# Attention and MLP in one kernel: batch 1's q exponentials by token tile, w1's sums in the raw weights' place, w2's differences in smaller parts, steps placed later

## The chip, the cores and the metric

The kernel runs on one core of a Trainium2 chip. The metric is the time on the device in microseconds (us), the median of a few runs. One execution was also taken by the hardware profiler. Engines are named as in its page: PE (TensorE), DVE (VectorE), ACT (ScalarE), POOL (GpSimd), SP (SyncE). Each runs its own queue of instructions in order; semaphores make one wait for another.

## The reference

```python
q_s = softmax(q, over the head's 64 columns)          # 8 batches, 8 heads, 576 tokens
k_s = softmax(k, over the 576 tokens)
kv  = einsum('bhsd,bhse->bhde', k_s, v)
x   = einsum('bhsd,bhde->bhse', q_s, kv)               # heads side by side: 8 x 576 x 512
xn  = (x - mean) / sqrt(var + 1e-06) * g_ln            # over the 512 columns
out = x + maximum(xn @ w_ch1, 0) @ w_ch2               # w_ch1 512 x 2048, w_ch2 2048 x 512
```

## The kernel before, in words

Each batch is worked on as 512 tokens in four token tiles (t = 0 to 3) of 128; the 64 tokens that remain of each of the eight batches form a ninth pass. A batch goes through the attention (exponentials of q and k on ACT, `kv_pairs` and `po_mm` on PE), a norm (`x_fast` on DVE gives x and xn; xn is transposed to xnT, on PE by `xn_pT` with a copy out of PSUM on ACT or DVE, or by DMA) and the MLP on PE.

Batch 0's MLP is the plain product (`mm1_part` into `ph`, `mm2_stream` into `pc`). Batch 1 does half of the first product in the plain way. All other products are a Strassen-Winograd scheme with seven products in place of eight (`mm1_fast`, products 1, 5, 6, 2, 7, 3, 4 into the banks bx, bb, bc; `mm2_fast` into ba, bb, bc, be). It needs sums of blocks: `sum_w1` of the first weight, `quarter_w2` (differences into w_q) of the second, `sum_x` (tq) of xnT and `sum_h` (hs) of the hidden layer. Product 4 of `mm1_fast` goes into the bank bx that `out_22` on DVE must have read.

The order of every engine's queue is written by hand. `run(main, side)` walks the list of a batch's MLP steps, each with a weight; a side step with place p is recorded as soon as the weights done reach p. In batch 0's list a matmul of 256 columns in the first product has 0.5, a `pc` matmul of the second has 1, which starts at 64; in batch 1's list all matmuls of 256 columns have 0.5. The attention of the next batch, its exponentials, casts and loads are such side steps, so a number in the code sets the place of a step in the queue of each engine that it uses.

Startup (`first_batch`): batch 0's keys are handled in 96-row tiles. For each pair of heads j, `kv0_mm(j)` multiplies on PE, writes `kv_sb[:, 0, j]` on DVE with its sum over the row, and from that sum `mbc[:, j]`, which `xT_mm(j, kh)` multiplies to take the mean off. `q0_rest(t)`, `x_fast(0, t)` and `xn_pT(0, t)` bring in token tiles 2 and 3 while the MLP of tiles 0 and 1 runs.

Loads of the first batches are issued by POOL, each waiting for the landing of the eighth before it: v and q of batch 0, w1 (`w1_sb`, named w_raw in the profile), half of w2 (w_sb), q1, k1, more of w2, v1 (vt, vr), ktr, the rest of w2, then batch 2. `scale_w1` makes w1g from w1_sb; batch 0's MLP reads w1_sb itself. `sum_w1` before writes into a tile of its own in the same memory, so that the first of the sums has to wait until all of w1_sb has been read:

```python
w1_sb = wts.tile([P, KO1, DH], BF16, tag="w1", name="w1_raw")
w1q["s"] = wts.tile([P, 4, 2, KO2 // 2, P], BF16, tag="w1", name="w1_q")
```

Exponentials of q for batches 1 to 7 (`exp_q(b, j, 4)`) take four heads of all four token tiles at once; `exp_qt(b, t)` takes one token tile of all heads. `eq_pT(1, t)` transposes token tile t of batch 1's q on PE, with the copy eqT on ACT; later batches are transposed by DMA from SP (`eq_T`, `xn_T`). PSUM has two pools: two banks for kv_pairs' and po's results, six for the rest.

Of the kernel before, what the change touches and what calls it, by code (L numbers as in the profile page):

```python
# [20 lines left out]
def kernel(  # L21
# [60 lines left out]
    g_one = const.tile([P, KO1], FP32)  # L82
    w1_sb = wts.tile([P, KO1, DH], BF16, tag="w1", name="w1_raw")
    w1g = const.tile([P, KO1, DH], BF16)
# [141 lines left out]

    w1q = {}

    def sum_w1(i, part):

        if not w1q:
            w1q["s"] = wts.tile([P, 4, 2, KO2 // 2, P], BF16, tag="w1", name="w1_q")
        ps = slice(4 * part, 4 * part + 4)
        blocks = w1g.rearrange("p (kh ko) (i odd n) -> p kh ko i odd n", kh=2, odd=2, n=P)
        a11, a12, a21, a22 = [blocks[:, kh, :, ps, odd, :] for odd in range(2) for kh in range(2)]
        s1, s2, s3, s4 = [w1q["s"][:, n, :, ps, :] for n in range(4)]
        dst, x, y, op = (
            (s1, a21, a22, ALU.add), (s2, s1, a11, ALU.subtract),
            (s4, a12, s2, ALU.subtract), (s3, a11, a21, ALU.subtract),
        )[i]  # L240
        for ko in range(2):
            nc.vector.tensor_tensor(out=dst[:, ko], in0=x[:, ko], in1=y[:, ko], op=op)
# [28 lines left out]
    def eq_T(c):  # L271
        dma_T(eqTs[c], eqs[c][0].rearrange("p t h d -> p (t h d)"), 0, T)
# [33 lines left out]
    def kv0_mm(j):  # L306
        pool, tag = (att_ps, "a") if j < 2 else (mm_ps, "m")
        pkv = pool.tile([P, P], FP32, tag=tag, name="pkv")
        for t in range(T0):
            lhsT, rhs, w = k0_mm(j, t)  # L310
            nc.tensor.matmul(pkv[:, 0:w], lhsT, rhs, start=(t == 0), stop=(t == T0 - 1))
        nc.vector.scalar_tensor_tensor(
            kv_sb[:, 0, j, :], in0=pkv, scalar=kvbox["rz"][:, j : j + 1], in1=diag,
            op0=ALU.mult, op1=ALU.mult, accum_out=kvbox["sum"][:, j : j + 1],
        )
        nc.vector.tensor_scalar(
            out=mbc[:, j], in0=ones_w, scalar1=-1.0 / DM, scalar2=kvbox["sum"][:, j : j + 1],
            op0=ALU.mult, op1=ALU.mult,
        )

# [204 lines left out]

    def quarter_w2(i, g):

        ks = slice(4 * g, 4 * g + 4)
        rows = [w2_sb[:, 8 * g + odd : 8 * g + 8 : 2, :] for odd in range(2)]
        (b11, b12), (b21, b22) = [(r[:, :, 0:DH2], r[:, :, DH2:DM]) for r in rows]  # L530
        t1, t2, t3, t4 = [w2_q[:, n, ks, :] for n in range(4)]
        dst, x, y = ((t1, b12, b11), (t3, b22, b12), (t2, b22, t1), (t4, b21, t2))[i]
        nc.vector.tensor_sub(out=dst, in0=x, in1=y)
# [164 lines left out]
    def prod1(n, g, dst, c, q, ko, first):  # L698

        i = 2 * g + q  # L700
        if n in (1, 2, 4):
            m, kh = {1: (2 * i, 0), 2: (2 * i, 1), 4: (2 * i + 1, 1)}[n]
            lhsT = w1g[:, 2 * kh + ko, m * P : m * P + P]
        else:
            lhsT = w1q["s"][:, {5: 0, 6: 1, 7: 2, 3: 3}[n], ko, i, :]
        if n in (1, 2, 3):
# [138 lines left out]
    def second_side():  # L845

        s = [(p, lambda i=i: quarter_w2(i, 1)) for i, p in enumerate((7.8, 7.9, 33.9, 66))]
        s += [(8.0, lambda: xn_pT(1, 3, nc.vector))]
        s += [(3, lambda: exp_q(2, 0, 4)), (7, lambda: exp_q(2, 2, 4)), (7.2, lambda: eq_T(2))]
        s += [(40, lambda: square_sum(1, 2)), (63, lambda: square_sum(1, 3)), (67, lambda: rstd_op(1))]  # L850
        s += [(10, lambda: load_batch(3, (2,), eqTs[2][0:1, T - 1, NP - 1, 0:4])), (31, lambda: load_batch(3, (0,)))]
        s += [(23 + j, lambda j=j: cast_v(2, j)) for j in range(2)]
# [4 lines left out]
        s += [(36, lambda: recip_q(2))]  # L857
        s += [(18, lambda: exp_k(2, 0, 4)), (22, lambda: exp_k(2, 2, 4)), (26, lambda: prep_kvrem(2))]
        s += [(35, lambda: kv_pairs(2))]
        s += [(40, lambda: start_x(2))]  # L860
        for t, (p0, p1) in enumerate(((42, 45), (47, 52.6), (55, 60.5), (65, 69))):
            s += spread([lambda t=t, i=i: po_mm(2, t, i) for i in range(NP)], p0, p1)
            s += [(p1, lambda t=t: x_fast(2, t)), ((69, 78, 84, 90)[t], lambda t=t: square_sum(2, t))]
        s += [(57, lambda: xn_T(2, 0, 2)), (73, lambda: xn_T(2, 2, 2)), (96, lambda: rstd_op(2))]
        s += [(74, lambda: exp_q(3, 0, 4)), (78, lambda: exp_q(3, 2, 4)), (84, lambda: eq_T(3))]
# [41 lines left out]
    def xn_pT(c, t, eng):  # L907
        pe_T(xnTs[c], xs[c][2][:, t], t, eng, None if c else g_col)
# [7 lines left out]
    def first_batch():  # L916
# [34 lines left out]
        nc.vector.memset(bones[64:P, 1:2], 1.0)  # L951
        nc.vector.memset(ones_w, 1.0)
        nc.vector.memset(diag, 0.0)
# [52 lines left out]
        eq_pT(0, 2, nc.scalar)  # L1006
        xT_mm(1, 1)
        eq_pT(0, 3, nc.vector)
        xT_mm(2, 1)
        xT_mm(3, 1)  # L1010
# [38 lines left out]
    with tc.manual_schedule(  # L1049
# [11 lines left out]
        def po_x(c, t):  # L1061
            for i in range(NP):
# [5 lines left out]
            [  # L1068
                (0, lambda: (q0_rest(2), x_fast(0, 2), x_normed(2))),
                (4, lambda: q0_rest(3)),  # L1070
                (4, lambda: (x_fast(0, 3), xn_pT(0, 2, nc.vector), x_normed(3))),
                (8, lambda: [po_mm(0, t, i) for t in range(2) for i in range(NP)]),
# [10 lines left out]
            ]  # L1083
            + [(62, lambda: exp_q(1, 0, 4)), (64, lambda: exp_q(1, 2, 4))]
            + [(67 + t, lambda t=t: reduce_q(1, t)) for t in range(T)]
            + [((74, 78, 86, 90)[t], lambda t=t: eq_pT(1, t, nc.scalar)) for t in range(T)]
            + [(78, lambda: nc.vector.reciprocal(eqs[1][2], eqs[1][1]))]
            + [(80, lambda: exp_k(1, 0, 4)), (84, lambda: exp_k(1, 2, 4))]
            + [(p, lambda i=i: scale_w1(i % KO1, i // KO1)) for i, p in enumerate((16, 18, 20, 22, 30, 32, 35, 37))]
            + [(p, lambda i=i: quarter_w2(i, 0)) for i, p in enumerate((46, 50, 54, 57))]  # L1090
            + [(98.5 + 0.4 * j, lambda j=j: cast_v(1, j)) for j in range(2)]
            + [(p, lambda i=i: sum_w1(i % 4, 1 - i // 4)) for i, p in enumerate((64, 65, 66, 66.5, 80, 84, 99.5, 118))]
            + [(100.4, lambda: prep_kvrem(1))]
            + [(103.5, lambda: (kv_pairs(1), start_x(1)))]
            + [(108.5, lambda: po_x(1, 0)), (110.5, lambda: po_x(1, 1))]
            + [(113.0, lambda: po_x(1, 2)), (114.9, lambda: xn_pT(1, 0, nc.scalar)), (115.9, lambda: square_sum(1, 0))]
            + [(115.9, lambda: po_x(1, 3)), (121.0, lambda: xn_pT(1, 1, nc.scalar)), (122.0, lambda: square_sum(1, 1))]
            + [(128.0, lambda: xn_pT(1, 2, nc.scalar))]

# [52 lines left out]
```

## Time and profile before

| | us |
|---|---|
| median of 3 runs | 264.96 (264.48 to 265.18) |
| the profiled execution: its time | 264.57 |
| its span in the profile | 262.8 |
| busy in it: PE, DVE, ACT, POOL | 255.6, 224.0, 174.3, 94.8 |
| granted PE clock | 0.998 |

A line of a timeline or a group gives the start (timelines), the busy time, the engine, the line of the kernel, the operation, out<-in by names, shapes and the count; in brackets stands the idle time before it and what ended it. PE's matmuls are pipelined with modelled ends, so their durations overlap: the distance from start to start tells the pace.

### The profile page before, as it was taken

How to read it: one execution, taken by the hardware profiler on the slowest of the kernel's cores; microseconds unless marked ns; L12 is line 12 of the kernel's file. 1: busy time of each engine (PE TensorE's matmuls, PEld its weight loads, DVE VectorE, ACT ScalarE, POOL GpSimd, SP SyncE). 2: the span in 40 equal slices, each digit the busy share in tenths (PEclk: the TensorE clock that was granted, in tenths of full speed). 3: DMA queues.
4: the chain of work that ended last, by engine and by line, in shares of the span. 5: the costliest groups of instructions: out<-in, count | busy, mean ns of one | idle time of the engine just before them, and what ended most of it. 6: DMA issues, size and time to landing. Idle time of an engine off the chain costs nothing.

```text
span 262.8 us, 6694 instructions
## 1 busy us (share of the span) xinstructions
PE 255.6 (97%) x2624; PEld 220.0 (84%) x2627; DVE 224.0 (85%) x492; ACT 174.3 (66%) x340; POOL 94.8 (36%) x148
## 2 busy tenths in 40 slices
PE   8999989999999999999999999999999999999993
PEld 6789745789888898999899889998899888888882
DVE  6879597999999999899889988998898869977872
ACT  4557780888977885789478947894788378447400
POOL 3962228233079104930980097009000800030000
PEclk9999999999999999999999999999999999999999
DMA  6999999979958995999299929994906320321014
GB/s 193 254 205 206 356 218 283 282 185 298 170 125 265 281 140 67 284 274 129 67 301 247 167 62 278 247 169 94 266 5 127 115 81 10 73 102 60 2 41 120
DMA packets 82536, 45.00 MB, mean 171 GB/s; under 512 B 58116, under 2 KB 79112, under 8 KB 82504
## 3 DMA queue, kind: packets, MB, share of 16 engines
q0 software_dynamic: 32464, 21.76, 44.2%
q1 hardware_dynamic: 49440, 22.29, 39.0%
q10 hardware_dynamic: 600, 0.53, 0.6%
q8 instruction: 20, 0.33, 0.5%
q14 instruction: 12, 0.10, 0.1%
HBM read 36.70 MB, written 9.44 MB: 176 GB/s over the span
## 4 chain that ended last, share of the span: by engine, by line
PE 82%; DMA 9%; POOL 3%; DVE 3%; ACT 1%; issue 0%; DVEq 0%
PE ba L566 21%; PE bx L711 20%; PE bb L711 10%; DMA qt<-in_q_dram 9%; PE be L566 5%; PE bc L566 5%; PE bb L566 5%; PE bc L711 5%; PE pc L519 3%; PE po L387 2%; PE pkv L357 2%; PE ph L483 1%; DVE x L427 1%; POOL w_raw L99 1%; DVE ot L500 1%; POOL v L965 1%
## 5 line engine op out<-in xcount | busy, mean ns | idle before, releaser
L566 PEld LDWEIGHTS <-hs 128*128 128x128 bf16 x512 | 49.8, 98 | 5.7
L711 PEld LDWEIGHTS <-w_q 128*128 128x128 bf16 x480 | 45.6, 98 | 5.1
L259 POOL TENSOR_TENSOR tq<-xnT 128x256 bf16<-128x256 bf16 x26 | 17.2, 677 | 77.0 <-DMA xnT<-xn 63.0
L566 PEld LDWEIGHTS <-hT 128*128 128x128 bf16 x384 | 37.1, 98 | 4.3
L711 PEld LDWEIGHTS <-w1g 128*128 128x128 bf16 x360 | 34.1, 98 | 4.1
L711 PE MATMUL bx<-tq,w_q 128*128 128x256 bf16 x240 | 31.7, 273 | 0.0
L566 PE MATMUL ba<-w_q,hs 128*128 128x256 bf16 x256 | 30.8, 273 | 0.0
L735 ACT COPY bc<-bx 128x512 f32<-128x512 f32 x30 | 16.7, 591 | 20.8 <-PE bx L711 20.5
L742 DVE TENSOR_TENSOR bb<-bx,s 128x512 f32<-128x512 f32 x30 | 19.5, 695 | 8.4 <-ACT s L739 5.7
L583 POOL DMA_DIRECT2D out_dram<-ot x28 | 15.4, 558 | 24.2 <-DVE ot L577 24.1
L427 DVE SCALAR_TENSOR_TENSOR x<-po,rq 128x512 bf16<-128x512 f32 x34 | 23.2, 683 | 0.9 <-PE po L387 0.7
L407 ACT ACTIVATE scrap<-x,mv 128x512 bf16<-128x512 bf16 x32 | 23.0, 720 | 1.4 <-DVE x L427 1.2
L753 ACT ACTIVATE hT<-bb 128x512 bf16<-128x512 f32 x30 | 16.3, 595 | 9.9 <-PE bb L711 9.1
L745 DVE TENSOR_TENSOR hT<-bx,s 128x512 bf16<-128x512 f32 x30 | 19.3, 684 | 3.8 <-PE bx L711 3.8
L387 PE MATMUL po<-kv_sb,eqT 128*128 128x128 bf16 x128 | 22.1, 219 | 0.0
L550 DVE TENSOR_TENSOR hs<-hT 128x1024 bf16<-128x1024 bf16 x32 | 21.6, 685 | 0.5 <-ACT hT L753 0.5
L753 ACT ACTIVATE hT<-bc 128x512 bf16<-128x512 f32 x30 | 16.4, 595 | 8.4 <-PE bc L711 8.4
L218 DVE TENSOR_REDUCE zq<-eq 128x16 f32<-128x1024 bf16 (+1 forms) x20 | 20.7, 1051 | 0.0
L591 ACT COPY s<-ba 128x512 f32<-128x512 f32 x15 | 8.7, 582 | 13.3 <-PE ba L566 8.6
L753 ACT ACTIVATE hT<-bx 128x512 bf16<-128x512 f32 x30 | 16.4, 604 | 0.7 <-PE bx L711 0.7
L566 PE MATMUL ba<-w_sb,hT 128*128 128x256 bf16 x128 | 16.7, 273 | 0.0
L739 ACT COPY s<-bb 128x512 f32<-128x512 f32 x30 | 16.5, 619 | 0.0
(152 smaller groups left out, 550.3 us busy)
## 6 DMA issues: line engine op xcount, KB each, us to landing
out_dram<-ot POOLq DMA_DIRECT2D x30, 256.0 KB, 5.0
qt<-in_q_dram SPq DMA_DIRECT2D x5, 1024.0 KB, 6.7
kt<-in_k_dram SPq DMA_DIRECT2D x5, 1024.0 KB, 12.2
qt<-in_q_dram POOLq DMA_DIRECT2D x2, 1024.0 KB, 12.4
kt<-in_k_dram POOLq DMA_DIRECT2D x2, 1024.0 KB, 14.1
vm<-in_v_dram POOLq DMA_DIRECT2D x16, 128.0 KB, 12.6
w_raw<-in_moe_w_ch_dram POOLq DMA_DIRECT2D x3, 512.0 KB, 10.4
w_sb<-in_moe_w_ch_dram POOLq DMA_DIRECT2D x3, 512.0 KB, 16.2
```

The source lines that it names most:

```text
L218: nc.vector.reduce_sum(eqs[c][1][:, ts], eqs[c][0][:, ts], axis=AX.X)
L259: eng.tensor_tensor(out=dst[:, t], in0=x[:, t], in1=y[:, t], op=ALU.subtract)
L387: nc.tensor.matmul(pobox["p"][:, i * P : i * P + P], eqTs[c][:, t, i, :], kv_sb[:, c, i, :], start=True, stop=True,)
L407: nc.scalar.activation(scrap, x[:, t], AF.Square, bias=mv[:, t, 0:1], scale=-float(DM), accum_out=mv[:, t, 1:2],)
L427: nc.vector.scalar_tensor_tensor(x[:, t].rearrange("p (h d) -> p h d", h=H), in0=pobox[c, t].rearrange("p (h d) -> p h d", h=H), scalar=1. ...
L550: nc.vector.tensor_tensor(out=dst, in0=x, in1=y, op=op)
L566: nc.tensor.matmul(hbox[bank][:, t], lhsT, rhs, start=first and (own or t == 0) and k == 0, stop=k == KH - 1, skip_group_check=True)
L711: nc.tensor.matmul(dst[:, q], lhsT, rhs, start=first and q == 0 and ko == 0, stop=ko == 1, skip_group_check=True)
L735: nc.scalar.copy(at[g, "c"], at[g, "x"])
L742: nc.vector.tensor_tensor(out=at[g, "b"], in0=at[g, "x"], in1=at[g, "s"], op=ALU.add)
L745: nc.vector.tensor_tensor(out=h_out(g, 1, 1), in0=at[g, "x"], in1=at[g, "s"], op=ALU.add)
L753: nc.scalar.activation(h_out(g, odd, half), at[g, name], AF.Relu)
```

## The change

- Batch 1's q exponentials become four `exp_qt(1, t)` in place of two `exp_q`; its first two transposes move one place later (74, 78 to 75, 79), the exponentials of k to 82 and 88.
- `sum_w1` writes into w1_sb: each set of four sums into that half of the raw columns that it does not come from. Eight sums are recorded at 42 to 53 and 66 to 84 in place of 64 to 84, 99.5 and 118.
- `quarter_w2` takes a first row and a count: rows 0 to 3 at 58 to 62 (before 46 to 57); rows 4 and 5 in batch 0's list at 99 to 102; rows 6 and 7 where before all of 4 to 7 stood.
- At startup `mbc` 0 to 2 go to ACT, 3 stays on DVE (ones_w now holds -1/512), `xT_mm(2, 1)` comes ahead of `eq_pT(0, 3)`, `q0_rest(2)` and what follows it move by 2, and `x_fast(0, 3)` moves behind `xn_pT(0, 2)`.
- Batch 1's `kv_pairs`, `po_x`, `xn_pT` and `square_sum` move to later places; the copy of `xn_pT(1, 3)` goes from DVE to ACT, at 6 in place of 8.
- In batch 1's list, steps of batch 2 move: the second halves of `exp_q` and `exp_k`, `eq_T`, `prep_kvrem`, `kv_pairs` (35 to 40), three of the `po_mm` groups with their `x_fast`, `xn_T`, and the load of batch 3's k (31 to 37).

The diff, without the parts that only rename:

```diff
-            w1q["s"] = wts.tile([P, 4, 2, KO2 // 2, P], BF16, tag="w1", name="w1_q")
+    def w1_sum(n, part):
+        at = DH // 2 * (1 - part)
+        return w1_sb[:, n, at : at + DH // 2].rearrange("p (ko i n) -> p ko i n", ko=2, n=P)
...
-        s1, s2, s3, s4 = [w1q["s"][:, n, :, ps, :] for n in range(4)]
+        s1, s2, s3, s4 = [w1_sum(n, part) for n in range(4)]
...
-        nc.vector.tensor_scalar(
-            out=mbc[:, j], in0=ones_w, scalar1=-1.0 / DM, scalar2=kvbox["sum"][:, j : j + 1],
-            op0=ALU.mult, op1=ALU.mult,
-        )
+        if j < NP - 1:
+            nc.scalar.activation(
+                mbc[:, j], ones_w, AF.Copy, scale=kvbox["sum"][:, j : j + 1]
+            )
+        else:
+            nc.vector.tensor_scalar_mul(
+                out=mbc[:, j], in0=ones_w, scalar1=kvbox["sum"][:, j : j + 1]
+            )
...
-    def quarter_w2(i, g):
+    def quarter_w2(i, k0, kn):
-        ks = slice(4 * g, 4 * g + 4)
-        rows = [w2_sb[:, 8 * g + odd : 8 * g + 8 : 2, :] for odd in range(2)]
+        ks = slice(k0, k0 + kn)
+        rows = [w2_sb[:, 2 * k0 + odd : 2 * (k0 + kn) : 2, :] for odd in range(2)]
...
-            lhsT = w1q["s"][:, {5: 0, 6: 1, 7: 2, 3: 3}[n], ko, i, :]
+            lhsT = w1_sum({5: 0, 6: 1, 7: 2, 3: 3}[n], i // 4)[:, ko, i % 4, :]
...
-        s = [(p, lambda i=i: quarter_w2(i, 1)) for i, p in enumerate((7.8, 7.9, 33.9, 66))]
-        s += [(8.0, lambda: xn_pT(1, 3, nc.vector))]
-        s += [(3, lambda: exp_q(2, 0, 4)), (7, lambda: exp_q(2, 2, 4)), (7.2, lambda: eq_T(2))]
+        s = [(p, lambda i=i: quarter_w2(i, 6, 2)) for i, p in enumerate((7.8, 7.9, 33.9, 66))]
+        s += [(6, lambda: xn_pT(1, 3, nc.scalar))]
+        s += [(3, lambda: exp_q(2, 0, 4)), (7.5, lambda: exp_q(2, 2, 4)), (7.6, lambda: eq_T(2))]
...
-        s += [(10, lambda: load_batch(3, (2,), eqTs[2][0:1, T - 1, NP - 1, 0:4])), (31, lambda: load_batch(3, (0,)))]
+        s += [(10, lambda: load_batch(3, (2,), eqTs[2][0:1, T - 1, NP - 1, 0:4])), (37, lambda: load_batch(3, (0,)))]
...
-        s += [(18, lambda: exp_k(2, 0, 4)), (22, lambda: exp_k(2, 2, 4)), (26, lambda: prep_kvrem(2))]
-        s += [(35, lambda: kv_pairs(2))]
+        s += [(18, lambda: exp_k(2, 0, 4)), (28.5, lambda: exp_k(2, 2, 4)), (33, lambda: prep_kvrem(2))]
+        s += [(40, lambda: kv_pairs(2))]
...
-        for t, (p0, p1) in enumerate(((42, 45), (47, 52.6), (55, 60.5), (65, 69))):
+        for t, (p0, p1) in enumerate(((47, 49), (51, 54), (57, 61), (65, 69))):
...
-        s += [(57, lambda: xn_T(2, 0, 2)), (73, lambda: xn_T(2, 2, 2)), (96, lambda: rstd_op(2))]
+        s += [(57.5, lambda: xn_T(2, 0, 2)), (73, lambda: xn_T(2, 2, 2)), (96, lambda: rstd_op(2))]
...
-        nc.vector.memset(ones_w, 1.0)
+        nc.vector.memset(ones_w, -1.0 / DM)
...
         xT_mm(1, 1)
+        xT_mm(2, 1)
         eq_pT(0, 3, nc.vector)
-        xT_mm(2, 1)
...
-                (0, lambda: (q0_rest(2), x_fast(0, 2), x_normed(2))),
+                (2, lambda: (q0_rest(2), x_fast(0, 2), x_normed(2))),
                 (4, lambda: q0_rest(3)),
-                (4, lambda: (x_fast(0, 3), xn_pT(0, 2, nc.vector), x_normed(3))),
+                (6, lambda: (xn_pT(0, 2, nc.vector), x_fast(0, 3), x_normed(3))),
...
-            + [(62, lambda: exp_q(1, 0, 4)), (64, lambda: exp_q(1, 2, 4))]
+            + [(62 + t, lambda t=t: exp_qt(1, t)) for t in range(T)]
...
-            + [((74, 78, 86, 90)[t], lambda t=t: eq_pT(1, t, nc.scalar)) for t in range(T)]
+            + [((75, 79, 86, 90)[t], lambda t=t: eq_pT(1, t, nc.scalar)) for t in range(T)]
...
-            + [(80, lambda: exp_k(1, 0, 4)), (84, lambda: exp_k(1, 2, 4))]
+            + [(82, lambda: exp_k(1, 0, 4)), (88, lambda: exp_k(1, 2, 4))]
...
-            + [(p, lambda i=i: quarter_w2(i, 0)) for i, p in enumerate((46, 50, 54, 57))]
+            + [(p, lambda i=i: quarter_w2(i, 0, 4)) for i, p in enumerate((58, 60, 61, 62))]
...
-            + [(p, lambda i=i: sum_w1(i % 4, 1 - i // 4)) for i, p in enumerate((64, 65, 66, 66.5, 80, 84, 99.5, 118))]
+            + [(p, lambda i=i: sum_w1(i % 4, 1 - i // 4)) for i, p in enumerate((42, 45, 50, 53, 66, 70, 80, 84))]
+            + [(99 + i, lambda i=i: quarter_w2(i, 4, 2)) for i in range(4)]
...
-            + [(103.5, lambda: (kv_pairs(1), start_x(1)))]
-            + [(108.5, lambda: po_x(1, 0)), (110.5, lambda: po_x(1, 1))]
-            + [(113.0, lambda: po_x(1, 2)), (114.9, lambda: xn_pT(1, 0, nc.scalar)), (115.9, lambda: square_sum(1, 0))]
-            + [(115.9, lambda: po_x(1, 3)), (121.0, lambda: xn_pT(1, 1, nc.scalar)), (122.0, lambda: square_sum(1, 1))]
-            + [(128.0, lambda: xn_pT(1, 2, nc.scalar))]
+            + [(110, lambda: (kv_pairs(1), start_x(1)))]
+            + [(p, lambda t=t: po_x(1, t)) for t, p in enumerate((114.8, 116.5, 118.6, 121))]
+            + [(p, lambda t=t: xn_pT(1, t, nc.scalar)) for t, p in enumerate((119, 122.5, 127.9))]
+            + [(p + 0.1, lambda t=t: square_sum(1, t)) for t, p in enumerate((119, 122.5))]
```

More of the change, by code (lines that the diff above doesn't have):

```diff
@@ L82 @@
     g_one = const.tile([P, KO1], FP32)
-    w1_sb = wts.tile([P, KO1, DH], BF16, tag="w1", name="w1_raw")
+    w1_sb = wts.tile([P, KO1, DH], BF16, name="w1_raw")
     w1g = const.tile([P, KO1, DH], BF16)
@@ L225, in scale_w1 @@
         )
-    w1q = {}
+    def w1_sum(n, part):
+        at = DH // 2 * (1 - part)
+        return w1_sb[:, n, at : at + DH // 2].rearrange("p (ko i n) -> p ko i n", ko=2, n=P)
     def sum_w1(i, part):
-        if not w1q:
-            w1q["s"] = wts.tile([P, 4, 2, KO2 // 2, P], BF16, tag="w1", name="w1_q")
         ps = slice(4 * part, 4 * part + 4)
```

## The prediction

> **What bounds the kernel.** I read the page, then the timeline of each engine up to 80 us, then the chain of waits from 30 to 60. The page says TensorE; its timeline gives the pitch.
>
> ```profile
> PE 255.6 (97%) x2624; PEld 220.0 (84%) x2627; DVE 224.0 (85%) x492; ACT 174.3 (66%) x340; POOL 94.8 (36%) x148
> ```
> ```profile
> 12.98 1.13 PE L328 MATMUL pxT<-eqT,mbc 128*128 128x256 bf16 x6 [0.18 <-DVE mbc L316]
> ...
> 33.45 0.28 PE L887 MATMUL ptr<-ident,eq 128*128 128x128 bf16 x2
> 34.40 0.28 PE L887 MATMUL ptr<-ident,eq 128*128 128x128 bf16 x2 [0.66 <-ACT eq L201]
> ```
> ```profile
> 68.20 1.91 PE L566 MATMUL ba<-w_q,hs 128*128 128x256 bf16 x16
> 69.94 1.91 PE L566 MATMUL bc<-w_sb,hT 128*128 128x256 bf16 x16
> ```
>
> Sixteen matmuls of 256 columns follow each other in 1.74 us: 0.109 each, so 0.217 for 512 columns and 0.055 for 128. From batch 2 on a batch takes 26.2 us with PE at this pitch; nothing can be won there. Where two PE starts lie further apart than the pitch, PE stood still: 0.35 and 0.29 before pxT (12.98, 13.72), 0.23 before xn's transposes (17.01), 0.24 and 0.83 before eq's (33.45, 34.40), 0.14 before po (43.75), 0.21 before ph (53.34). That is 2.29 us, and no more can be gained. PE gets the same matmuls after the change.
>
> ```profile
> 32.34 2.00 ACT L201 ACTIVATE eq<-qt 128x1024 bf16<-128x1024 f32 x2 [1.36 <-DMA qt<-in_q_dram]
> ...
> 41.06 0.42 ACT L187 ACTIVATE ekr<-ktr 128x256 bf16<-128x256 f32 x1 [1.63 <-DMA ktr<-in_k_dram]
> ```
> ```profile
> 11.98 0.25 DVE L316 TENSOR_SCALAR mbc<-ones_w,kvs 128x128 bf16<-128x128 bf16 x1
> ...
> 12.53 0.39 DVE L316 TENSOR_SCALAR mbc<-ones_w,kvs 128x128 bf16<-128x128 bf16 x1
> ...
> 13.09 0.57 DVE L316 TENSOR_SCALAR mbc<-ones_w,kvs 128x128 bf16<-128x128 bf16 x1
> ...
> 29.82 0.69 DVE L533 TENSOR_TENSOR w_q<-w_sb 128x1024 bf16<-128x1024 bf16 x1 [3.11 <-DMA w_sb<-in_moe_w_ch_dram]
> ...
> 62.47 1.28 DVE L745 TENSOR_TENSOR hT<-bx,s 128x512 bf16<-128x512 f32 x2
> ```
> ```profile
> 52.95 0.35 DVE xnT L893
> 53.30 0.04 issue
> 53.34 3.65 PE ph L483 x32
> ```
>
> ACT's rows show q1 and k1's rest bound by their loads; DVE's, the unequal price of mbc and an idle 3.11 us; the chain, PE waiting for the last xnT copy, queued on DVE behind 1.40 of w_q.
>
> **A, startup.** Three of the four mbc leave DVE for ACT, idle from 10.3 to 12.67. No row has this copy on ACT: 256 and 512 elements take 0.42 and 0.60, so about 0.33 for 128 (bounds 0.25, DVE's, and 0.42). mbc 0 then ends at 11.77, 0.1 later; but the kv_sb steps follow each other, kv_sb 3 starts at 12.55, when PE has its product, and mbc 3 at 12.94. If that lasts 0.26, xT_mm(3,0) starts at 13.28 in place of 13.72 (gain 0.44); if it ends with POOL's DMA issue at 13.64, as the 0.57 did, the gain is 0. I take 0.40 for mbc 3, between its rows: 0.31.
> The Trainium skill (SBUF — State Buffer, Who interferes with whom) says that a GpSimd instruction and a DVE tensor_scalar in a two-port mode exclude each other for a whole instruction. The trace agrees in part: POOL issued DMAs without a gap from 10.60 to 14.38, and two of the four mbc still took 0.25. By that rule the gain is 0 and the sum below 0.81 (264.15).
> Part goes back: q0_rest(2) moves behind four matmuls (0.44), so z_q(2) starts at 15.71 less the gain. From z_q(2) to xn_pT(0,2) the DVE chain takes 1.74 as before (15.27 to 17.01): 17.45. x_fast(3) now waits behind its copy (transpose to copy 0.42, pitch 0.61: 18.48), and xn(3) ends 1.07 later at 19.55: xn_pT(0,3) at 19.61 in place of 19.46, a loss of 0.15. Together +0.16, bounds -0.15 and +0.29.
>
> **B, q1's exponentials.** The load ends at 32.32 either way. Two instructions over half the heads (1.06 each) become four over a token tile (0.63, pitch 0.52 by L209). Tile 0 is ready at 32.97; its transposes, one pc later, are due at 31.06 + 11 x 0.217 = 33.45. Both stalls go: 1.07. The four end at 34.53 (0.2 later); the eqT copies and exp_k behind them on ACT end by 38.8, before ekr, which has to wait for ktr to 41.06. Bounds 0.9 (A's gain brings the transposes nearer to 32.97) and 1.07; I take 1.02, for 0.05 comes back where xn_pT(1,0) now follows po directly.
>
> **C, work on DVE.** w1's sums are the same 16 instructions of 0.38. The first eight enter the idle 3.11 us: the raw half that they overwrite was last read by PE at 25.8, and the relu ahead of them in DVE's queue (26.03) waits for that matmul anyway. The first quarter_w2 start at 30.0, after w_sb's landing, and end at 32.5; four reduces end at 36.2, the last sums at 38.5, v1's casts (landing 40.16) at 40.6, four differences of 512 elements (0.35) at 42.05. What is split costs DVE 0.06 each. PE waits for none of it: 0.
>
> **D, kv_pairs(1) and batch 1's xn.** kv_pairs(1) moves behind six more pc. It starts at 41.76 - 1.07 + 1.30 - 0.16 = 41.83; ekr ends at 41.48, so a cover of 0.35 remains, and what ktr loses beyond it PE loses one for one. rzk follows at 42.8, DVE free since 42.05. To po the way is 1.99 as before, with its 0.14. The first ph of batch 1 follows 6.39 after kv_pairs' start (0.76, 18 pc 3.91, four po 0.88, three transposes 0.66, waits 0.14 and 0.05), at 48.2 in place of 49.41. xn_pT(1,3)'s copy moves to ACT, whose queue starts its first xnT copy 4.0 after kv_pairs and by its rows (copies 0.49, squares 0.81, exp_q 0.95, relu 0.48) has the last one done at 9.1; ph needs it at 10.1. Ahead of it stands exp_q(2,0): q2 landed at 46.0, the exponential is due at 48.9. If that cover goes, the copy and ph wait with it. The 0.21 goes (bounds 0 and 0.21).
>
> **E, batch 2's steps.** kv_pairs(2) moves from weight 35 to 40, x_fast(2,0) from 45 to 49, just ahead of out_22, which product 4 waits for. From PE's last pkv to product 4 there are now products 6, 2, 7 and 3 and eight po: 32 x 0.109 + 8 x 0.055 = 3.93. In the same time DVE has rzk and kv_sb to do (1.18 by 42.52 to 43.70), two adds (1.24), x_fast and xn (1.00), out_22 (0.68), all one behind the other, and 0.05 passes until PE sees it: 4.15, and 0.61 more for the second out_22, for which PE has 0.55 more. Before, PE took 5.10 (58.34 to 63.44), and out_22 was done at 63.15 (row L745: 62.47, 1.28 for two). New stall 0.22 + 0.06, so 0.27; bounds 0 (the DVE rows shrink by 5%) and 0.45 (a queue entry ahead of rzk that is late by 0.2). exp_k(2,2,4) and ekr move behind two more relus on ACT, the last of which waits for PE: ekr ends 14.8 after kv_pairs(1)'s start, and kv_pairs(2) needs it at 15.35; the seed copies behind it on ACT have 1.0.
> k3's load (31 to 37) issues behind exp_k(2), q3 and eq_T(2) on SP; it landed at 69.43 for a use at 72.43: 0. The order within POOL's and SP's queues stays.
>
> **Sum.** 0.16 + 1.02 + 0.21 - 0.27 = 1.12. The profiled execution (264.57: span 262.8 and 1.77 around it) becomes 263.45; the median, 0.39 above it, 263.84.
>
> **Rivals.**
> 1. Everything pays: mbc 3 at 0.26, no stall in E: 0.29 + 1.02 + 0.21 = 1.52, so 263.4. For it: two mbc of 0.25 beside POOL. Against: DVE's chain in E adds up to more than PE's.
> 2. POOL holds mbc 3 to 13.64 and E costs 0.45: -0.15 + 1.02 + 0.21 - 0.45 = 0.63, 264.3.
> 3. The change doesn't do what it says at q1: the load lands later by as much as PE comes earlier, or ACT's four tiles hold eqT back; PE's stall moves from the transposes to kv_pairs(1) waiting for ekr. Left: about 0.2, 264.75. Against: ekr's cover of 0.35.
> 4. Slower: DVE, now busy from 26.7 without a gap, keeps POOL from issuing (vr, ktr at 27.7 to 32.6), and ktr lands late. Issue to landing was 8.4 for the last ktr, so an issue must slip by 8 us before a landing moves; from 0.35 past that PE loses all, and at 2.3 the kernel is slower by 0.8: 265.8 and up. Against: under DVE's load after 30.0 POOL's issues took 0.62 to 0.72, as at 27.74 (0.61).
> The Trainium skill (same page and section) says that tensor_tensor does not stop descriptor writing; those rows agree.
>
> **How the numbers follow.** Forecast 0.50, rivals 0.13, 0.20, 0.09, 0.08. A measurement here tells 0.3% (0.79 us) from no change. Faster: forecast, rival 1 and a quarter of rival 2, 0.68; same 0.24; slower 0.08. The bounds give 0.30 to 1.57 (264.66 to 263.39); with 0.2 for the spread of runs, and rival 3 inside, 263.2 to 264.9.
>
> **What would show it.** Right: no PE gap at the eq transposes near 33.3; kv_pairs(1) near 41.8; batch 1's first ph near 48.2; no wait for xnT(1,3); DVE idle gone at 27; a gap of 0.1 to 0.4 before product 4; 26.2 us per batch after it. Wrong: PE waiting for ekr or casts at kv_pairs(1), a POOL issue or landing that moved, or any new gap over 0.5.

## The result, and the profile after

The changed kernel is slower: 265.62 us median of 20 runs against 264.78 of 20 runs of the kernel before, ratio 1.0042 (95% interval 1.0026 to 1.0057). The prediction said 263.84, faster. The profiled execution took 265.36 (span 263.5), 0.79 more than the one before. In some executions startup is later by about 1 us (kv_pairs(1) near 42.7 instead of 41.7), so kernels are compared by the ratios of their medians, and single profiles stretch by stretch.

PE's busy share is as before:

```profile
PE 256.4 (97%) x2627; PEld 220.7 (84%) x2627; DVE 224.8 (85%) x492; ACT 176.5 (67%) x346; POOL 94.9 (36%) x148
```

PE's timeline after the change, at the places of the old gaps and at a new one (start, busy, engine, line, operation; in brackets the idle time before it and what ended it):

```profile
33.35 0.39 PE L891 MATMUL ptr<-ident,eq 128*128 128x128 bf16 x4
33.57 1.03 PE L523 MATMUL pc<-w_sb,hT 128*128 128x512 bf16 x4
34.43 0.39 PE L891 MATMUL ptr<-ident,eq 128*128 128x128 bf16 x4
...
55.68 1.04 PE L715 MATMUL bx<-xnT,w1g 128*128 128x256 bf16 x8
56.55 0.60 PE L715 MATMUL bb<-tq,w_raw 128*128 128x256 bf16 x4
58.56 0.60 PE L715 MATMUL bb<-tq,w_raw 128*128 128x256 bf16 x4 [1.41 <-DVE hT L496]
```

The eq transposes stand in PE's pace: no gap. The first bx of batch 1 starts at 55.68, where it started at 56.83: up to here PE is 1.15 ahead. Then product 5 stops between its two banks. Four matmuls after 56.55 the next was due at 56.99 and started at 58.56, 1.57 late. It waits for a relu (the maximum with 0) on DVE that empties the bank. Counted by the pace, PE's gaps now are 0.99 in startup (0.87 before), 0 at the eq transposes (1.07), 0.35 around batch 1's po and xn (0.19), 0 before ph's third tile (0.21), 1.57 at product 5 (0), 0.35 from 62.41 to 64.72 (0): 0.9 more in all, about what the executions differ by.

The chain of waits from 48 to 60 says how DVE came to be late:

```profile
51.18 2.87 DVE w_q L537 x2
54.05 2.25 DVE zq L218 x2
...
57.90 0.61 DVE hT L496
...
58.56 0.60 PE bb L715 x4
```

Two w_q differences of 512 elements hold 2.87 us of the path. Elsewhere such a pair takes 0.75. DVE's and POOL's timelines side by side, first of the changed kernel:

```profile
51.10 2.95 DVE L537 TENSOR_TENSOR w_q<-w_sb 128x512 bf16<-128x512 bf16 x2
53.97 2.33 DVE L218 TENSOR_REDUCE zq<-eq 128x16 f32<-128x1024 bf16 x2
...
57.83 0.68 DVE L496 TENSOR_SCALAR hT<-ph 128x512 bf16<-128x512 f32 x1
```
```profile
50.87 1.30 POOL L259 TENSOR_TENSOR tq<-xnT 128x256 bf16<-128x256 bf16 x2
52.13 1.29 POOL L259 TENSOR_TENSOR tq<-xnT,tq 128x256 bf16<-128x256 bf16 x2
```

and of the kernel before:

```profile
51.47 1.48 DVE L533 TENSOR_TENSOR w_q<-w_sb 128x1024 bf16<-128x1024 bf16 x2
52.88 0.41 DVE L893 COPY xnT<-ptr 128x512 bf16<-128x512 bf16 x1
53.21 2.33 DVE L218 TENSOR_REDUCE zq<-eq 128x16 f32<-128x1024 bf16 x2
...
57.08 0.68 DVE L492 TENSOR_SCALAR hT<-ph 128x512 bf16<-128x512 f32 x1
```
```profile
51.11 0.68 POOL L259 TENSOR_TENSOR tq<-xnT 128x256 bf16<-128x256 bf16 x1
53.37 0.67 POOL L259 TENSOR_TENSOR tq<-xnT 128x256 bf16<-128x256 bf16 x1 [1.57 <-DVE xnT L893]
53.99 1.30 POOL L259 TENSOR_TENSOR tq<-xnT,tq 128x256 bf16<-128x256 bf16 x2
```

Before, POOL did one tq subtraction and then waited 1.57 for DVE's copy of the last xnT tile, behind both w_q. So POOL's other three met DVE's reduces, which took their usual 1.2 each. After, the copy is done early on ACT; POOL runs its four in a row from 50.87 to 53.42, and DVE's first w_q, issued at 51.10, ends at 53.71, just after the row (2.62; the second took 0.41). The reduces, casts and relus behind it are late by as much.

That alone does not account for 1.57. In the kernel before, PE came to the same bank later:

```profile
57.58 0.32 PE L357 MATMUL pkv<-vm,ek 128*64 128x65 bf16 x8
...
58.57 1.04 PE L711 MATMUL bb<-tq,w_q 128*128 128x256 bf16 x8
```

There kv_pairs(2), from 57.58 to 58.34, stood ahead of product 5, whose second bank was due at 59.01, four matmuls after 58.57. The relu was done at 57.75, so it had 1.2 to spare. After the change the relu is done at 58.51, 0.75 later, and PE is due at 56.99, 2.02 earlier: 1.15 by the stalls that went, and 0.87 because step E put kv_pairs(2) behind product 5. By these rows a change that left kv_pairs(2) where it was would have stalled there for about 0.7 (an estimate; it was not run).

### The profile page after: what moved, and what is told of

Read it like the earlier page. It is cut to its first block, busy times and chain, and to the rows that moved or that the text cites. A ratio compares the mean times of both kernels' runs of the same rounds, so it can differ in the third digit from the quotient of the medians.

```text
span 263.5 us, 6700 instructions
## 1 busy us (share of the span) xinstructions
PE 256.4 (97%) x2627; PEld 220.7 (84%) x2627; DVE 224.8 (85%) x492; ACT 176.5 (67%) x346; POOL 94.9 (36%) x148
## 4 chain that ended last, share of the span: by engine, by line
PE 92%; DVE 6%; issue 0%; ACT 0%; DVEq 0%
PE ba L570 21%; PE bx L715 20%; PE bb L715 10%; PE ph L487 5%; PE bb L570 5%; PE bc L570 5%; PE be L570 5%; PE bc L715 5%; PE pc L523 4%; PE warm L820 3%; PE po L391 3%; PE pkv L361 2%; DVE w_q L537 1%; DVE ot L504 1%; DVE x L431 1%; PE ptr L891 1%
## 5 line engine op out<-in xcount | busy, mean ns | idle before, releaser
L715 PEld LDWEIGHTS <-w_raw 128*128 128x128 bf16 x480 | 45.6, 98 | 6.8 <-issue 1.6
L715 PE MATMUL bx<-tq,w_raw 128*128 128x256 bf16 x240 | 31.5, 273 | 0.0
L715 PE MATMUL bb<-tq,w_raw 128*128 128x256 bf16 x120 | 15.7, 272 | 1.4 <-DVE hT L496 1.4
```

The lines of the kernel that those rows point to most:

```text
L715: nc.tensor.matmul(dst[:, q], lhsT, rhs, start=first and q == 0 and ko == 0, stop=ko == 1, skip_group_check=True)
```

## The experiments: the collision

Theory 1: DVE's w_q is kept out while POOL runs subtractions that read SBUF. Rivals: the pair is slow by its new shape or operands (theory 2); or PE's stall comes from the moved steps of batch 2 or ACT's new order (theory 3). Ratios are to the kernel before, run beside each.

**w2_later**, the changed kernel with the pair moved on DVE:

```diff
-        s = [(p, lambda i=i: quarter_w2(i, 6, 2)) for i, p in enumerate((7.8, 7.9, 33.9, 66))]
+        s = [(p, lambda i=i: quarter_w2(i, 6, 2)) for i, p in enumerate((24.2, 24.4, 33.9, 66))]
```

> The changed kernel with one edit: the first two w_q differences of batch 1's list (2.95 us in the changed kernel's trace, where 0.75 was due) are recorded at 24.2 and 24.4 instead of 7.8 and 7.9, behind the two reduces and the two casts on DVE, so that POOL's four tq differences of two inputs each (50.87 to 53.4) meet the reduces, which read one. PE, ACT, POOL and SP keep their order. Theory 1 (collision: a DVE subtraction of two SBUF inputs is kept out while POOL runs its own): the pair takes 0.75 at the new place, the second relu of ph starts near 56.0 instead of 57.83, PE's stall of 1.57 before bb at 58.56 goes: 1.4 to 1.6 faster than the changed kernel, 263.9, some 0.3% faster than before. Theory 2 (the pair is slow by itself, by its new shape of 128x512 or by its operands): 2.95 at the new place too, the stall stays or grows, no gain. Theory 3 (PE's stall comes from the moved steps of batch 2 or the new ACT order, DVE being late only beside it): the pair may be short, but the stall stays over 1 us, gain under 0.5.

The pair took 0.75; ratio 1.0001 (0.9984 to 1.0017). PE still waited 0.45 at product 5's second bank: with the pair gone, the reduces came up against the second exp_q of batch 2 on ACT (0.97 idle), and the pair now stood ahead of the second relu. Theory 2 is out; part of the stall has a second cause behind the first.

**tq_on_dve**, the pair left in place and POOL's work taken away:

```diff
-        if c == 1 and i > 1:
+        if c == 1:
```

> The changed kernel with one edit: batch 1's first two tq differences, which POOL does as four instructions of 256 elements, are done by DVE as two of 512 (0.41 each by its rows for the other two). The pair of w_q stays where it is. Theory 1 (collision with POOL): the w_q pair takes 0.75 in its old place, as POOL has nothing to subtract; DVE has 0.82 more to do, and 2.2 less to wait; the relu before product 5's second bank starts near 56.6, PE's stall falls from 1.57 to between 0 and 0.3: 1.2 to 1.5 faster than the changed kernel, 264.0. Theory 2 (slow by itself): 2.95 as before plus 0.82, so 0.8 slower than the changed kernel, 266.2. Theory 3 (moved steps): no change beyond 0.3.

The pair took 0.75 in its old place, PE's stall fell to 0.17; ratio 0.9988 (0.9970 to 1.0006), 0.5% under the changed kernel. Theory 1 holds from both sides, for the pair and for most of the stall. Theory 3 has a share in it, the 0.87 by which E brought PE to product 5 earlier: in the kernels below that have E taken back, PE does not wait at product 5 at all.

**copy_alone**, the kernel before with one line of the change:

```diff
-        s += [(8.0, lambda: xn_pT(1, 3, nc.vector))]
+        s += [(6, lambda: xn_pT(1, 3, nc.scalar))]
```

> The kernel before with one edit: the copy of batch 1's last xnT tile goes from DVE at 8.0 to ACT at 6, nothing else of the change. This copy is what held POOL's last three tq differences back to 53.37, behind DVE's w_q pair. Theory 1 (collision): POOL now runs its four tq in a row from 51.1 to 53.7, DVE's w_q pair (1.48 for two of 1024 elements) is held and ends near 54.3 instead of 52.9, the reduces, casts and relus behind it are late by 1.0 to 1.5, and PE waits 0.8 to 1.3 for a relu before product 5; its stall of 0.21 before ph goes: 0.5 to 1.1 slower than before, 265.3 to 265.9. Rival (the prediction's own step D): the stall of 0.21 goes and nothing is held: 0.2 faster than before. Theory 3 (moved steps of batch 2): as the rival, since they are not moved here.

A miss: ratio 0.9996 (0.9983 to 1.0009). POOL's timeline shows why:

```profile
52.30 0.68 POOL L259 TENSOR_TENSOR tq<-xnT 128x256 bf16<-128x256 bf16 x1
53.39 0.68 POOL L259 TENSOR_TENSOR tq<-xnT 128x256 bf16<-128x256 bf16 x1 [0.41 <-ACT xnT L889]
54.03 1.74 POOL L259 TENSOR_TENSOR tq<-xnT,tq 128x256 bf16<-128x256 bf16 x2
```

In this kernel ACT's copy came 0.41 after POOL's first subtraction. In that gap DVE got its turn, and then it was POOL's third that waited (1.11 instead of 0.66). The pair took 1.96 instead of 1.48, and PE did not wait: without steps B and E it came to product 5's second bank at 59.99, 0.82 after the relu's end at 59.17. So a collision need not cost PE anything. The changed kernel has two things that this one lacks: an unbroken row on POOL, and a PE that comes earlier.

**tq_twice** doubles POOL's work, **copy_pair** changes what DVE does:

```diff
-        for t in range(2):
+        for t in (0, 0, 1, 1) if c == 1 else range(2):     # tq_twice
...
+        if k0 == 6 and i < 2:                              # copy_pair
+            nc.vector.tensor_copy(out=dst, in_=x)
+            return
```

copy_pair leaves two differences out, so its w_q holds other numbers; it serves for the time of the copies alone.

> The changed kernel with POOL's four tq subtractions each done twice (same operands, same result), so a row of eight, 5.2 us, in place of four, 2.6. Collision: DVE's first w_q gets its turn only when POOL's row is over, so it takes 5.2 instead of 2.62, the relus behind it are later by 2.6, and PE's stall before product 5's second bank grows from 1.57 to about 4.1: 2.6 slower than the changed kernel. Rival (DVE's instruction is only slowed to a share of the memory's rate while POOL works, or is long by itself): with 2.62 for 2.3 us of overlap it would have got its 0.38 of work done in a fixed time, so it stays at 2.62 and the kernel within 0.3 of the changed one.

> The changed kernel with the two w_q instructions that collide turned into copies of one operand, 128x512 bf16 from and to SBUF; the two differences are left out, so w_q's rows 6 and 7 hold the wrong numbers. It tells which instructions of DVE POOL's row keeps out. If only those of two SBUF inputs: the copies take 0.25 to 0.4 each beside POOL's tq (the reduces of one input took their usual 1.2 beside them), PE's stall of 1.57 goes to 0 or near it, 1.4 to 1.6 faster than the changed kernel. If fast copies between SBUF tiles are kept out as well: the first lasts to the end of POOL's row, 2.5, and nothing is gained.

tq_twice missed both expectations: with twice the work on POOL the pair took 1.42, not 5.2 and not 2.95, and PE's stall fell to 0.86; ratio 1.0022 (0.9994 to 1.0050).

```profile
50.69 1.42 DVE L537 TENSOR_TENSOR w_q<-w_sb 128x512 bf16<-128x512 bf16 x2
```

POOL's second instruction writes what its first wrote, and started 0.08 after the first had ended; from there on the two engines took turns. In copy_pair (1.0018, 0.9998 to 1.0038) POOL's row was unbroken again, and the copies fared hardly better than differences (PE stood 1.17):

```profile
51.09 2.54 DVE L538 COPY w_q<-w_sb 128x512 bf16<-128x512 bf16 x2
```

The first copy took 2.34, the second 0.28. The Trainium skill (SBUF — State Buffer, Who interferes with whom) says that DVE shares a port pair with GpSimd, that an instruction of two SBUF inputs contends with a GpSimd instruction that reads SBUF, that copies can in their two-port modes, and that tensor_reduce never does on this chip. The rows agree on the last three: 2.62 for the difference, 2.34 for the copy, 1.21 for the reduce beside POOL's subtractions (tq_order, below).

**tq_order** changes only the order of POOL's four:

```diff
+        if c == 1:
+            for t in range(2):
+                eng.tensor_tensor(out=t1[:, t], in0=b12[:, t], in1=b11[:, t], op=ALU.subtract)
+                eng.tensor_tensor(out=t2[:, t], in0=b22[:, t], in1=t1[:, t], op=ALU.subtract)
+            return
...
-        s += [(at, lambda i=i: sum_x(1, i)) for i, at in enumerate((9.1, 9.2, 31.5, 36))]
+        s += [(at, lambda i=i: sum_x(1, i)) for i, at in ((0, 9.1), (2, 31.5), (3, 36))]
```

> The changed kernel with one edit: POOL's same four tq subtractions in another order, each token half's second difference right behind its first, which it reads, instead of both first differences and then both second ones. The w_q pair stays where it collides. In tq_twice each repeated instruction started 0.08 after the end of the one before, and DVE got its turns (0.61 and 0.89 for the pair); in the changed kernel the four overlapped by 0.04 and DVE got none for 2.6. If a gap in POOL's row is what lets DVE in: the pair takes 1.0 to 1.6 instead of 2.95, PE's stall before product 5 falls from 1.57 to 0.4 to 0.9, 0.7 to 1.1 faster than the changed kernel, ratio to the kernel before 1.001. If POOL keeps its right through dependent instructions as well: 2.95 and 1.57 as before, ratio 1.004.

Ratio 0.9963 (0.9949 to 0.9977): 0.37% faster than the kernel before, where the change is 0.42% slower. POOL and DVE:

```profile
50.87 0.68 POOL L260 TENSOR_TENSOR tq<-xnT 128x256 bf16<-128x256 bf16 x1
51.63 0.74 POOL L261 TENSOR_TENSOR tq<-xnT,tq 128x256 bf16<-128x256 bf16 x1
52.34 0.84 POOL L260 TENSOR_TENSOR tq<-xnT 128x256 bf16<-128x256 bf16 x1
53.26 0.67 POOL L261 TENSOR_TENSOR tq<-xnT,tq 128x256 bf16<-128x256 bf16 x1
```
```profile
50.93 1.73 DVE L542 TENSOR_TENSOR w_q<-w_sb 128x512 bf16<-128x512 bf16 x2
52.58 2.33 DVE L218 TENSOR_REDUCE zq<-eq 128x16 f32<-128x1024 bf16 x2
```

POOL's second instruction reads what the first wrote and so starts 0.08 after its end. DVE gets in after one: the pair takes 1.73 and is done at 52.66 instead of 54.05. PE waits 0.35 at product 5. That an unbroken row on POOL is what keeps DVE out is shown. The gain was larger than expected (1.001): the profiled executions are 1.16 apart (264.20 against 265.36), about what the stall lost, but the medians 1.72 (263.90 against 265.62), and where the rest comes from is not shown.

## The experiments: the parts of the change

Against tq_order, where little collides, each part was taken back by itself: its lines of the change's diff, reversed, of which these are the first.

```diff
-            + [(62 + t, lambda t=t: exp_qt(1, t)) for t in range(T)]     # order_q_by_heads
+            + [(62, lambda: exp_q(1, 0, 4)), (64, lambda: exp_q(1, 2, 4))]
...
-        if j < NP - 1:                                                   # order_start_back
...
-        s += [(40, lambda: kv_pairs(2))]                                 # order_kv2_back
+        s += [(35, lambda: kv_pairs(2))]
```

> tq_order with step B taken back: q1's exponentials by four heads in two instructions, its first transposes at 74 and 78. Step B as predicted: PE waits for the second exponential again, until 2.06 after the load's landing (34.40 - 32.34 in the kernel before); tq_order's PE came to the transposes at 33.14 and its load at 32.06, so 0.9 to 1.0 slower than tq_order, ratio to the kernel before about 1.000. In runs in which startup puts PE later, less is lost: 0.4 to 1.0 in the median, 0.998 to 1.000. Rival (the time goes to a later wait in any case): within 0.2 of tq_order.

> tq_order with step A taken back: mbc on DVE for all four pairs, xT_mm(2,1), q0_rest(2) and x_fast(0,3) at their places in the kernel before. The prediction's step A: 0.16 slower than tq_order, ratio 0.997. By the Trainium skill's rule, as the prediction weighed it (SBUF — State Buffer, Who interferes with whom), step A is worth 0 less what goes back, so this kernel is the same or 0.15 faster. More than 0.3 either way: something else in startup decides.

> tq_order with step E taken back: batch 2's second exp_k, prep_kvrem, kv_pairs, po groups, x_fast, first xn_T and k3's load at their places in the kernel before. Step E as predicted: 0.27 faster than tq_order (its profile shows 0.43 + 0.05 before product 4), 0.3 to 0.4 by that profile; ratio 0.995. Rival: po of batch 2 waits instead (0.34 and 0.35 before po at 58.8 in the kernels that took E back), or xnT of batch 2 is late: no gain, 0.996 to 0.998.

**order_q_by_heads**: 1.0012 (0.9996 to 1.0027), 0.5% over tq_order. PE stands again:

```profile
33.34 0.28 PE L896 MATMUL ptr<-ident,eq 128*128 128x128 bf16 x2
34.26 0.28 PE L896 MATMUL ptr<-ident,eq 128*128 128x128 bf16 x2 [0.65 <-ACT eq L201]
```

From PE's first transpose of batch 0's q (behind its warm-up) to kv_pairs(1) it takes 35.49, tq_order 34.40: 1.09 for step B. **order_start_back**: 0.9978 (0.9962 to 0.9995), its interval overlaps tq_order's; the same stretch takes 34.41, so step A is worth 0.0 in the profiles. **order_kv2_back**: 0.9981 (0.9966 to 0.9996), not faster. From kv_pairs(1) to product 4 it takes 20.22, tq_order 21.29: that is 1.07 less. Not all of it is E's: tq_order's additional waits are 0.25 at batch 1's xn transposes, ahead of everything that E moves (one xn on DVE took 0.57 instead of 0.35), 0.35 at product 5 and 0.54 from there to product 4. But 15 us later order_kv2_back loses it again:

```profile
77.49 1.03 PE L720 MATMUL bb<-tq,w_raw 128*128 128x256 bf16 x8 [0.65 <-POOL tq L264]
78.74 1.03 PE L720 MATMUL bx<-tq,w_raw 128*128 128x256 bf16 x8 [0.22 <-ACT s L748]
```

POOL's tq of batch 2 wait for xnT, which the second DMA transpose landed at 75.98 (74.70 in tq_order): 1.20 of gaps by the pace. kv_pairs(3) comes 40.24 after kv_pairs(1), in tq_order 40.25.

**q1_alone** is the kernel before with B and batch 1's moved steps of D, the copy left on DVE (the change's own lines):

```diff
+            + [(62 + t, lambda t=t: exp_qt(1, t)) for t in range(T)]
...
+            + [(110, lambda: (kv_pairs(1), start_x(1)))]
```

> The kernel before with two parts of the change alone: batch 1's q exponentials by token tile with its transposes and k's exponentials at their new places, and kv_pairs(1), po_x, xn_pT and square_sum of batch 1 at theirs. The copy of xn_pT(1,3) stays on DVE, w1's sums, w2's differences, startup and batch 2's steps stay as before. The prediction's step B: PE's stalls of 0.24 and 0.83 before q1's transposes go, kv_pairs(1) starts near 42.0 behind ekr at 41.5, the stall of 0.21 before ph stays: 1.0 faster than before (0.8 to 1.1), 263.8. Rival: what PE gains it loses again at kv_pairs(1) (ktr's load lands as late as before, DVE's sums end later than the casts need): under 0.4 faster. By theory 1 nothing new collides here, as POOL's tq still wait for DVE's copy.

Ratio 1.0015 (0.9996 to 1.0034); the rival's number, by a wait that neither named. The gap at the eq transposes went, and PE stood before ph:

```profile
53.37 0.81 PE L483 MATMUL ph<-xnT,w1g 128*128 128x256 bf16 x6 [1.14 <-DVE xnT L893]
```

1.30 by the pace, for a copy that ends at 53.31 behind the w_q pair, as it did before. What B wins, PE loses here unless the copy moves too: with B in place that move is worth 1.30, not 0.21. This rests on one kernel, whose output is wrong (0.055 off, relative) for a cause that is not known: it may lack a wait that it should have, so its time is weaker evidence than the others'.

**mended** is tq_on_dve with two more edits, **mended_q_by_heads** the same with B taken back:

```diff
-        s = [(p, lambda i=i: quarter_w2(i, 6, 2)) for i, p in enumerate((7.8, 7.9, 33.9, 66))]
+        s = [(p, lambda i=i: quarter_w2(i, 6, 2)) for i, p in enumerate((57, 70, 71, 80))]
...
-            s += [(p1, lambda t=t: x_fast(2, t)), ...
+            s += [((52, 54, 61, 69)[t], lambda t=t: x_fast(2, t)), ...
```

> The changed kernel with three edits: batch 1's tq differences all on DVE (as in tq_on_dve, 0.12% under the kernel before there); the four w_q differences of rows 6 and 7 out of DVE's crowded stretch, to 57, 70, 71 and 80, where only the second product reads them; x_fast(2,0) at 52 instead of 49, behind out_22. Expected by the collision and step E as the prediction had it: no PE stall at product 5's second bank (1.57 in the changed kernel, 0.17 in tq_on_dve), none before product 4 (0.24 in the changed kernel). That is 1.8 less than the changed kernel, 0.9 to 1.0 less than the kernel before: 263.7, ratio 0.9965 (0.995 to 0.998). If something else in the new order costs the rest of the shortfall (startup, ACT's order at batch 1), the ratio stays at 0.9988 or above.

> The kernel of mended with q1's exponentials taken back: two exp_q over four heads each, and the first two transposes at 74 and 78. Step B as predicted: PE stands 0.24 + 0.83 before the transposes again, all that follows is later by it: 1.0 slower than mended (0.8 to 1.1, ratio to mended 1.004). Rival (what PE gains at q1 it only waits for later, at kv_pairs(1), behind ktr's load, or at batch 1's first copies on DVE): under 0.4 between the two.

mended: 1.0042 (1.0025 to 1.0059). Both old stalls were gone, and my places made two new ones: 0.76 before a po at 63.05, whose bank x_fast empties, and this, for a w_q that the second product reads:

```profile
69.83 1.25 PE L570 MATMUL ba<-w_q,hs 128*128 128x256 bf16 x10 [1.36 <-DVE w_q L537]
```

mended_q_by_heads: 1.0063 (1.0042 to 1.0084). Its load of q1 had landed by 31.76, and PE's gap at the transposes was 0.47, not 1.07: B is worth the distance from PE's arrival to 2.06 behind that landing, so its size depends on the run.

## The experiments: what is late next

**pair_32** moves the pair behind both relus; **pair_32_kv2_back** takes E back as well, **pair_32_kv2_start_back** also A; **tq_dve_kv2_back** is tq_on_dve without E:

```diff
-        s = [(p, lambda i=i: quarter_w2(i, 6, 2)) for i, p in enumerate((7.8, 7.9, 33.9, 66))]
+        s = [(p, lambda i=i: quarter_w2(i, 6, 2)) for i, p in enumerate((32, 32, 33.9, 66))]
```

> The changed kernel with the colliding w_q pair at 32, on DVE behind both relus of ph that product 5 waits for (in w2_later it stood ahead of the second one, and PE still waited 0.45). PE, ACT, POOL and SP keep their order. Collision alone: POOL's row meets only the reduces, both relus are out by 57.3, product 5's second bank is free when PE comes; no stall there. 1.6 faster than the changed kernel, 0.45 faster than w2_later: ratio to the kernel before 0.998 (0.996 to 0.9995). Rival (the reduces, which wait for the second exp_q of batch 2 behind the xnT copy on ACT, hold the relus in any case): a stall of 0.4 stays, ratio 1.000.

> pair_32 with step E undone: batch 2's second exp_k, prep_kvrem, kv_pairs, po groups, x_fast, first xn_T and the load of batch 3's k at the places that they have in the kernel before. Step E as predicted costs 0.27: the stalls of 0.19 + 0.05 before product 4 and 0.11 at product 7 go, and nothing else comes: 0.3 faster than pair_32 (ratio to the kernel before 0.997). Rival: with PE earlier, kv_pairs(2) now comes ahead of the casts of v or of ekr and waits there by as much (that is what the later place was good for): no gain, or up to 0.5 slower.

> pair_32_kv2_back with step A undone as well: mbc on DVE for all four, xT_mm(2,1), q0_rest(2) and x_fast(0,3) at their places in the kernel before. What is left of the change is B, C and D with the pair moved. If step A was worth the predicted 0.16, this is 0.16 slower than pair_32_kv2_back; if it was worth nothing, as the gaps of the changed kernel's profile add up (0.99 against 0.87 before), the same or 0.1 faster; more than 0.3 either way would be a surprise. B and D together then give 1.02 + 0.21 less what comes late next: ratio to the kernel before 0.9955 to 0.998.

> tq_on_dve (no subtraction on POOL for batch 1, so no collision anywhere) with step E undone. Its profiled run had 1.4 of PE waiting at batch 2's tq, behind xnT by DMA (landed 76.7, against 74.0 before), which came behind the loads of batch 3. If the later place of kv_pairs(2) and of k3's load brought that, it goes, with 0.24 before product 4: 0.3 to 1.0 faster than tq_on_dve, ratio to the kernel before 0.995 to 0.998. Rival (the transposes by DMA are a limit of their own, which PE meets once it is earlier than before by 1.2): batch 2's tq late again, ratio 0.999 as for tq_on_dve.

Ratios in this order: 1.0005 (0.9984 to 1.0026), 0.9987 (0.9970 to 1.0004), 0.9992 (0.9974 to 1.0011), 0.9984 (0.9968 to 1.0001). In pair_32 product 5 no longer waits, product 4 starts at 62.16 instead of 64.13, and batch 2 then loses most of it (PE, then POOL):

```profile
78.06 1.03 PE L715 MATMUL bb<-tq,w_raw 128*128 128x256 bf16 x8 [1.24 <-POOL tq L259]
```
```profile
76.72 1.29 POOL L259 TENSOR_TENSOR tq<-xnT 128x256 bf16<-128x256 bf16 x2 [14.08 <-DMA xnT<-xn]
```

xnT landed at 76.55, in the changed kernel at 74.10. Four profiles show this wait (tq_on_dve, pair_32, tq_dve_kv2_back, order_kv2_back); pair_32_kv2_back does not, and its profiled execution took 263.60. Two tries at the transposes, on pair_32_kv2_back: **one_xnT** joins them in one, **pe_xnT** does tiles 2 and 3 on PE.

```diff
-        s += [(57, lambda: xn_T(2, 0, 2)), (73, lambda: xn_T(2, 2, 2)), ...
+        s += [(73, lambda: xn_T(2, 0, 4)), ...                             # one_xnT
+        s += [(57, lambda: xn_T(2, 0, 2)), (84, lambda: xn_pT(2, 2, nc.scalar)),
+              (90, lambda: xn_pT(2, 3, nc.scalar)), ...                    # pe_xnT
```

> pair_32_kv2_back with batch 2's two DMA transposes of xn joined into one of all four tiles, at the place of the second (73). If the early first transpose, which runs among the loads of batch 3's k and v, is what draws the second one out (3.2 to 3.6 us on SP each in the stalled profiles, 1.2 to 2.2 in the others): the joint one is issued near 69, lands before 75, PE does not wait at batch 2's tq, and the long half of the runs goes: median 263.6, ratio 0.9965. If DMA transposes behind those loads are the limit by themselves: it lands at 76 or later, PE waits 1 to 2 at batch 2's tq in every run, ratio 1.000 to 1.004.

> pair_32_kv2_back with batch 2's xn tiles 2 and 3 transposed on PE (8 transposes of 128 columns, 0.055 each, at 84 and 90) and copied on ACT (0.49 each), in place of the second DMA transpose. PE has 0.44 more to do. If the late xnT by DMA is what costs the other half of the gain: no wait at batch 2's tq, the spread of the runs shrinks, median 263.4 + 0.44 = 263.9, ratio 0.997 to 0.998. If that wait is not what lengthens the runs: 0.44 slower than pair_32_kv2_back, ratio 1.000.

0.9991 (0.9972 to 1.0010) and 1.0010 (0.9992 to 1.0027). Neither profile shows the wait, yet the runs of both spread over 1.9 to 2.6 us like those of their base, and pe_xnT is slower than its base by 0.6, the matmuls that it adds being 0.44. (pe_xnT's output is wrong too, 0.057 off, cause unknown.) So the wait is real where it shows, but it does not by itself explain the spread; pe_xnT's profile has startup late by 1.0 (kv_pairs(1) at 42.68 against 41.71). What makes the second transpose land 2 us later in some executions stays open.

## Why the prediction was wrong, by its steps

- **C failed, and with it D.** The sum has no term for the wait that decided. C says: "What is split costs DVE 0.06 each. PE waits for none of it: 0." It priced a w_q of 512 elements at 0.35 and only by what stands ahead of it on DVE. The row "[1.57 <-DVE xnT L893]" on POOL was in the trace of before: POOL's tq read the xnT tile whose copy D moves. D followed that copy's place on ACT and the 0.21 of ph; it did not ask what else reads the tile. The pair measured 2.95 instead of 0.75, the relu before product 5 was late, and PE stood 1.57. The kernels in which the pair is not held, or held less, are 0.4 to 0.8% faster than the changed kernel (w2_later, tq_on_dve, tq_order).
- **The place for the slower case was wrong.** Rival 4 had DVE keeping POOL from issuing DMAs, with ktr late. ktr landed at 41.30 (40.97 before, with startup 0.22 later), ekr ran from 41.38 to 41.80, and kv_pairs(1) started at 41.89 (41.83 predicted) without waiting for it. It was POOL that kept DVE out, 10 us later.
- **B was right**: no gap at the transposes, 1.09 against 1.02 by order_q_by_heads. Whether it reaches the end depends on what waits next: by kv_pairs(3) the profiles of order_q_by_heads and tq_order are only 0.34 apart, since tq_order's PE waits more on the way, and without the copy's move nothing was left (q1_alone, with its doubt).
- **A was mis-sized**: 0.16 predicted, 0.0 measured, inside its bounds. The copies on ACT took 0.40 each (0.33 estimated), 0.34 from start to start, mbc 3 0.45 (0.40 taken), but gaps of 0.27 and 0.33 stayed before pxT. The Trainium skill's rule, weighed there, also gave 0; these runs do not show that it is for its reason.
- **D's other parts**: the first ph of batch 1 at 48.47 (48.2 predicted); 0.16 more than before at xn's transposes, the 0.21 gone.
- **E was right at product 4 and failed at product 5.** From 62.41 to 64.72 the changed kernel's PE stands 0.35 (0.27 predicted, to 0.45). But E counted from PE's last pkv on and did not ask what kv_pairs(2) had covered ahead of it: the relu before product 5's second bank, by 0.87. In tq_order 0.35 + 0.54 of PE's waits lie where E's steps do, yet taking E back did not gain (order_kv2_back); in that profile batch 2's xnT came late. E's place does not decide that: PE waited for xnT in two profiles with E in place (tq_on_dve, pair_32) and in two without (tq_dve_kv2_back, order_kv2_back).

## What to carry to other kernels

When a copy moves to another engine, list every reader of its result and see where each of them will now run, not only the one that waited. Where VectorE's copies or two-input operations and GpSimd's run over SBUF data at the same time, look at the rows of both side by side: a long row of GpSimd instructions without a gap is the costly case, and another order of the same instructions can be most of the cure. A step that moves behind a consumer no longer covers that consumer's wait: kv_pairs(2) cost PE the same time in both places, but in the old one a relu ended meanwhile. A gain early in a chain is worth no more than the cover of what comes next (the time by which it is ready before it is needed), so price the next reader's landing before counting it.

## What the hardware showed beyond expectation

POOL kept DVE out not for one instruction but for its whole row of four (2.62 us for 0.38 of work), where each started 0.03 to 0.05 before the end of the one before. The Trainium skill (SBUF — State Buffer, Who interferes with whom) says, of a DVE instruction in a two-port mode, that the one that issues first has the shared ports for the whole instruction; these rows, of an instruction with two SBUF inputs, show that POOL's right can pass on to its next instruction while DVE waits. With a gap of 0.08 in the row (tq_twice, tq_order) DVE got in after one. The order of arrival does not explain both: in the changed kernel POOL's second to fourth were issued after DVE's w_q (51.10) and went ahead of it, while in tq_twice POOL's third, which also started 0.04 before its second ended, gave way to a w_q that had come before it. What decides there was not settled.
